# Early tokens' second matmul placed in the front, banks for second matmuls, and job DMAs on the sync queue, in an attention and mixture-of-experts kernel

## The chip, the cores and the metric

The kernel runs on one core of one Trainium2 chip. The metric is the device time of one execution in microseconds (us). Engines are named as in the profile: PE (TensorE matmul), PEld (TensorE weight load), DVE (VectorE), ACT (ScalarE), POOL (GpSimd), SP (SyncE); a "q" behind a name (PEldq, ACTq, SPq) means the sequencer, which issues DMAs and does branches and register loads.

## What is computed

The reference, cut to what matters:

```python
def _attn_ref(q, k, v):                      # (8 batches, 8 heads, 576 tokens, 64)
    q_s = softmax(q, axis=-1); k_s = softmax(k, axis=2)
    kv = np.einsum('bhsd,bhse->bhde', k_s, v)
    return np.einsum('bhsd,bhde->bhse', q_s, kv)

def _moe_ref(x, w_gate, w_output_gate, w1, w2):   # x: 4608 x 512, 8 experts, F = 1024
    e_idx = np.argmax(x @ w_gate, axis=1)
    gate_w = softmax(x @ w_gate)[arange, e_idx]; eom = sigmoid(x @ w_output_gate)
    for e in range(8):
        mask = e_idx == e
        ye = np.maximum(x[mask] @ w1[e], 0.0) @ w2[e]
        out[mask] = gate_w[mask, None] * eom[mask, e, None] * ye

def _moe2_ref(x, w_in, w_out):                    # 512 -> 2048 -> 512
    r = np.maximum(x @ w_in, 0.0)
    return (r * r) @ w_out

x = attn_out.transpose(0, 2, 1, 3).reshape(4608, 512)
return _moe2_ref(_moe_ref(x))
```

## The kernel before, in words

Three stages follow each other. The **front** (`front`, L84 to L560) computes the attention batch by batch and routes each token to one expert (`route_a`, `route_b`, `scatter`); the tokens go to `xd` in DRAM, and their places, ordered by expert, to `idl` and then `idbin`. The first 384 tokens that an early count gives to expert 0 ("early tokens") are gathered before the routing is finished, and their first matmul is done in the front (`early_mm`). At its end `window_sums` and `window_place` write the table `tab` (L621): for each of 19 windows its expert, its first token, its width (3: 384 columns, 2: 256, 0: none), and whether the next window changes the expert. All engines then read `tab` into registers (L634) and branch on it (`tc.If`).

The **windows** (`run`, `slot`, L766 to L945): slots 0 to 4 are skipped here, slots 5 to 18 run. A slot does, in this order: the first half of the second matmul (`mm2`, L695, 48 matmuls) of the window before; the transposes of its own tokens (`prep`, L675); the gather of the next window's tokens on POOL (L703); a few "ticks"; the second half of mm2; the output copies on ACT (`out_`, L858) and their stores; then its own first matmul (`mm1`, L681, 8 groups of 12) with `hook` after each group; then the scaling of the next tokens on POOL (`scale`, L700); at a change of expert the split of the next w1 (`split_w1`) and the load of its w2. A split (L630 on ACT, L631 on DVE) makes two fp32r parts, high and rest, of one fp32 tensor, so each product takes three passes. The load of w1 and the split of w2 stand in the hook after group 2. In this run experts begin at slots 5 (the early one), 7, 9, 10, 12 and 14; the widths of slots 5 to 18 are 384, 384, 384, 256, 256, 384, 256, 384, 256, 384, 384, 384, 384, 256.

**Ticks** (`tick`, L804) turn w_in and w_out from a 64-bit form into fp32, 64 jobs of 256 columns. Job j's data comes by `job_load` (256 KB into one of four `cv_s`); DVE does six operations (L818 to L827) on `ca` and `cb`, POOL one (L825), ACT a Square (L810); a job goes through ticks j and j+1. The first 32 jobs (w_in) are then stored to `wid_d` (L806), in tick j+2; the other 32 become `wO` in SBUF. Slots 7 to 12 have six ticks, slots 13 to 18 five: three (two) between the halves of mm2, three in the hooks after groups 1, 4 and 6. Loads and stores of jobs are issued on ACT's queue; SP's queue issues the weight loads.

**PSUM**: eight banks. mm1's groups and mm2's four outputs take turns in five of them, and `prep` uses the other three:

```python
pm = bank[(12 * i + f) % 5]                               # mm1, group f of slot i
pm = [bank[(12 * i + 8 + c) % 5] for c in range(KC)]      # mm2
```

The **end** (L946 to L1000) is the dense second layer, from `yd`, twelve times 384 tokens.

The order in each engine's queue is the order in which the program issues: nothing reorders it. What the change touches is the end of `front`, `early_mm`, `job_load`, `tick`, `mm1`, `mm2`, `out_` and `slot`.

## Time and profile before

| | us |
|---|---|
| median of 3 runs | 1545.45 (1543.21 to 1545.7) |
| the profiled execution | 1553.64 |
| its span | 1551.8 |
| PE busy | 1439.6 (93%) |
| DVE busy | 657.5 (42%) |
| ACT busy | 499.3 (32%) |
| POOL busy | 304.2 (20%) |

The mean granted clock of PE is 0.964 of full speed. Times inside the trace count from the start of the span. The span is 1.8 us shorter than its own execution's time, and that execution is 8.2 us longer than the median of the runs. Busy time of PE is modelled: consecutive groups of matmuls overlap by some tenths of a us, so the distance from one start to the next is the better duration.

### The profile page before, as it was taken

How to read it: one execution, taken by the hardware profiler on the slowest of the kernel's cores; microseconds unless marked ns; L12 is line 12 of the kernel's file. 1: busy time of each engine (PE TensorE's matmuls, PEld its weight loads, DVE VectorE, ACT ScalarE, POOL GpSimd, SP SyncE). 2: the span in 40 equal slices, each digit the busy share in tenths (PEclk: the TensorE clock that was granted, in tenths of full speed). 3: DMA queues.
4: the chain of work that ended last, by engine and by line, in shares of the span. 5: the costliest groups of instructions: out<-in, count | busy, mean ns of one | idle time of the engine just before them, and what ended most of it. 6: DMA issues, size and time to landing. Idle time of an engine off the chain costs nothing.

```text
span 1551.8 us, 21664 instructions
## 1 busy us (share of the span) xinstructions
PE 1439.6 (93%) x8180; PEld 1352.8 (87%) x8180; DVE 657.5 (42%) x1302; ACT 499.3 (32%) x1004; POOL 304.2 (20%) x315
## 2 busy tenths in 40 slices
PE   6999649998678799999999999999999999999998
PEld 6888549998678789999999999999999999999997
DVE  4455651267555666444532434223343232433322
ACT  4566421233333334333522323222232222322222
POOL 1244641134224265443000000000000000000000
PEclk9999879999889899999999999999999999999999
DMA  8564624367675746332520101001010100100000
GB/s 311 187 242 182 165 76 97 48 200 152 179 191 121 192 121 145 103 102 51 149 69 14 42 0 41 19 23 41 1 42 0 41 34 8 41 1 21 8 15 21
DMA packets 62220, 135.61 MB, mean 87 GB/s; under 512 B 13360, under 2 KB 31920, under 8 KB 58096
## 3 DMA queue, kind: packets, MB, share of 16 engines
q1 hardware_dynamic: 31200, 79.13, 15.9%
q10 hardware_dynamic: 22752, 32.99, 9.1%
q0 software_dynamic: 8112, 21.47, 4.5%
q8 instruction: 91, 1.49, 0.4%
q14 instruction: 65, 0.53, 0.1%
HBM read 98.36 MB, written 35.20 MB: 86 GB/s over the span
## 4 chain that ended last, share of the span: by engine, by line
PE 75%; DMA 4%; DVE 2%; issue 2%; ACT 1%; ACTq 0%; POOL 0%; POOLq 0%; DVEq 0%; PEldq 0%
PE bank L972 26%; PE bank L993 25%; PE bank L681 12%; PE bank L695 11%; DMA wid_d<-cv_a 3%; DMA raw<-moe_w 1%; PE bank L675 1%; DVE wA L631 1%; ACT yb L858 0%; DVE cv_a L819 0%; POOL xr L700 0%; DVE cv_b L824 0%; DMA out<-xr,idt 0%; DVE cv_a L827 0%; ACTq L799 0%
## 5 line engine op out<-in xcount | busy, mean ns | idle before, releaser
L993 PE MATMUL bank<-wO,h 128*128 128x512 f32 x1728 | 396.5, 390 | 0.0
L993 PEld LDWEIGHTS bank<-wO,h 128*128 128x128 f32 x1728 | 324.1, 188 | 66.4
L695 PE MATMUL bank<-h,wB 128*128 128x384 f32 (+1 forms) x1440 | 236.9, 324 | 24.4 <-issue 20.5
L681 PE MATMUL bank<-xT,wA 128*128 128x384 f32 (+1 forms) x1344 | 221.2, 328 | 35.8 <-ACT yb L858 26.2
L695 PEld LDWEIGHTS bank<-h,wB 128*128 128x128 f32 x1440 | 230.4, 195 | 25.7 <-issue 21.8
L681 PEld LDWEIGHTS bank<-xT,wA 128*128 128x128 f32 x1344 | 218.1, 199 | 37.1 <-ACT yb L858 27.5
L975 ACT ACTIVATE r<-bank 128x384 f32<-128x384 f32 x192 | 94.4, 492 | 443.2 <-PE bank L972 443.2
L977 DVE TENSOR_TENSOR gg<-r 128x384 f32<-128x384 f32 x192 | 107.3, 559 | 286.4 <-ACT r L975 286.2
L972 PE MATMUL bank<-xT,wB 128*128 128x384 f32 x1152 | 201.9, 334 | 0.0
L972 PE MATMUL bank<-xT,wA 128*128 128x384 f32 x1152 | 201.8, 336 | 0.0
L972 PEld LDWEIGHTS bank<-xT,wB 128*128 128x128 f32 x1152 | 200.3, 188 | 0.9
L972 PEld LDWEIGHTS bank<-xT,wA 128*128 128x128 f32 x1152 | 200.0, 188 | 1.0
L998 POOL DMA_INDIRECT out<-xr,idt x36 | 35.0, 974 | 770.9 <-DVE xr L997 765.9
L631 DVE TENSOR_TENSOR h<-gg,h 128x384 fp32r<-128x384 f32 x192 | 107.3, 559 | 111.5 <-ACT h L630 111.5
L630 ACT CAST h<-gg 128x384 fp32r<-128x384 f32 x192 | 98.7, 514 | 122.6 <-DVE gg L977 122.6
L685 DVE SCALAR_TENSOR_TENSOR h<-bank,h 128x384 fp32r<-128x384 f32 (+1 forms) x112 | 55.5, 506 | 103.2 <-ACT h L689 99.6
L825 POOL TENSOR_TENSOR cv_b<-cv_b,cv_e 128x256 f32<-128x256 f32 x64 | 52.6, 822 | 235.7 <-DVE cv_b L824 235.4
L997 DVE COPY xr<-bank 128x512 f32<-128x512 f32 x36 | 24.9, 692 | 123.7 <-PE bank L993 123.7
L689 ACT ACTIVATE h<-bank 128x384 fp32r<-128x384 f32 (+1 forms) x112 | 49.3, 452 | 79.0 <-PE bank L681 74.7
L810 ACT ACTIVATE cv_s<-cv_s 128x256 f32<-128x256 f32 x64 | 28.3, 443 | 117.8 <-DMA wid_d<-cv_a 45.4
L631 DVE TENSOR_TENSOR xT<-bank,xT 128x512 fp32r<-128x512 f32 x42 | 26.5, 683 | 85.8 <-ACT xT L630 85.8
L703 POOL DMA_INDIRECT xr<-xd,wid x45 | 44.6, 992 | 88.1 <-issue 71.3
(171 smaller groups left out, 1203.4 us busy)
## 6 DMA issues: line engine op xcount, KB each, us to landing
raw<-moe_w SPq DMA_DIRECT2D x52, 512.0 KB
yd<-yb ACTq DMA_DIRECT2D x56, 192.0 KB
raw<-yd SPq DMA_DIRECT2D x11, 768.0 KB
v<-v SPq DMA_DIRECT2D x8, 1024.0 KB
q<-q SPq DMA_DIRECT2D x8, 1024.0 KB
cv_s<-moe_w_in ACTq DMA_DIRECT2D x32, 256.0 KB
cv_s<-moe_w_out ACTq DMA_DIRECT2D x32, 256.0 KB
kt<-k SPq DMA_DIRECT2D x7, 1152.0 KB
```

Of the source, the lines that this page charges most:

```text
L630: nc.scalar.copy(out=hi, in_=src)
L631: (eng or V).tensor_tensor(out=lo, in0=src, in1=hi.bitcast(F32), op=ALU.subtract)
L681: nc.tensor.matmul(out=pm, lhsT=wA[a][:, c, f * P:(f + 1) * P], rhs=xT[b][:, c, 0:n], start=c == 0 and (a, b) == (0, 0), stop=c == KC - 1 ...
L685: V.scalar_tensor_tensor(out=h[1], in0=pm, scalar=0.0, in1=h[0].bitcast(F32), op0=ALU.max, op1=ALU.subtract)
L689: nc.scalar.activation(out=h[0], in_=pm, func=AF.Relu)
L695: nc.tensor.matmul(out=pm[c], lhsT=wB[a][:, f, c * P:(c + 1) * P], rhs=h[b], start=f == 0 and (a, b) == (0, 0), stop=f == 7 and a == 1)
L703: nc.gpsimd.indirect_dma_start(out=xr[j], out_offset=None, in_=xd[0:n], in_offset=bass.IndirectOffsetOnAxis(ap=wid[i % 2][:, j:j + 1], axi ...
L825: G.tensor_tensor(out=b.bitcast(F32), in0=b.bitcast(F32), in1=ce.bitcast(F32), op=ALU.subtract)
L972: nc.tensor.matmul(out=pm, lhsT=wi(a, 8 * hf + f)[:, c], rhs=yhl[b][:, c], start=c == 0 and (a, b) == (0, 0), stop=c == KC - 1 and a == 1)
L975: nc.scalar.activation(out=r, in_=pm, func=AF.Relu)
L977: V.tensor_tensor(out=gg, in0=r, in1=r, op=ALU.mult)
L993: nc.tensor.matmul(out=pm, lhsT=g[a][f][:, u * P:(u + 1) * P], rhs=wO[b][:, 8 * hf + f, :], start=hf == 0 and f == 0 and (a, b) == (0, 0), ...
```

## The change

It has four parts. In the front, the pieces of the w1 and w2 splits are issued in other places, the early tokens' transposes and first matmul earlier, in banks of the pool of `pt` tiles, and their second matmul (96 matmuls into four new banks `acc`) before the register loads of `tab`. In the slots, mm2 always writes the four `acc` banks, mm1 takes turns in the other four, and `prep` in three of those; no slot does the early window's mm2. Loads and stores of jobs go to SP's queue, `ca` has four buffers, `b` is written in place in `cv_s`, `ce` has two buffers, the store of a job is issued in tick j+1 instead of j+2, and loads three ahead instead of two. The scaling of the next tokens comes before mm1 instead of after it.

```diff
@@ front, from batch 6 on @@
         x_mm(n, 1)
         kv_m(n + 1)
         x_t(n, 3)
+        moe.split_w1([0], V)
         x_mm(n, 2)
+        moe.split_w1([1], V)
         x_mm(n, 3)
...
+        moe.split_w1([2], V)
         route_b(full)
-        moe.split_w1([0], V)
         x_mm(n, 1)
+        x_t(n, 3)
         route_b2(full)
         scatter(full)
-        x_t(n, 3)
-        route_a(late)
-        moe.split_w1([1], V)
+        moe.split_w1([3], V)
+        moe.load_w2(0)
         x_mm(n, 2)
         x_t(n, 4)
-        route_a1(late)
-        route_a2(late)
-        moe.split_w1([2, 3], V)
+        route_a(late)
         rctx.close()
         moe.open_down()
         moe.early_open()
-        moe.load_w2(0)
+        moe.early_prep(ps_t)
         x_mm(n, 3)
+        route_a1(late)
+        x_mm(n, 4)
+        route_a2(late)
...
+        moe.open_acc()
+        em, st = moe.early_mm(ps_t)
+        em(1)
+        route_a(last)
+        em(1)
...
         route_b(late)
         route_b2(late)
         scatter(late)
-        moe.early_prep(ps_t)
-        x_mm(n, 4)
-        moe.split_w2([0], V)
...
-        window_sums(tc, scratch, cst, pc, spec, wq)
+        moe.split_w2([0], V)
         em(1)
         st(1)
...
+        window_sums(tc, scratch, cst, wt_cnt, spec, wq)
         st(1)
-        moe.split_w2([1, 2, 3], V)
+        moe.split_w2([1], V)
+        em(1)
+        window_place(tc, scratch, cst, wq, tab, lambda: None)
+        em(1)
+        moe.split_w2([2, 3], V)
         moe.gather(MAXW)
+        em(6)
         regs = moe.regs()
@@ early_mm @@
+    def open_acc():
+        ap = octx.enter_context(tc.tile_pool(name="m_acc", bufs=1, space=PSUM, side="right", reuse_waits="tile"))
+        acc.extend(ap.tile([P, 512], F32, name=f"acc{i}") for i in range(KC))
...
+            for f in range(8):
+                mm2_f(f, [x[:, 0:EW] for x in acc], [h[f] for h in hT])
                 yield
@@ run: banks and buffers @@
-        bank.extend(ps.tile([P, 512], F32, name=f"bank{i}") for i in range(8))
+        bank.extend(ps.tile([P, 512], F32, name=f"bank{i}") for i in range(4))
+        bank.extend(acc)
...
-            ca = [cv.tile([P, CW], I32, name=f"cv_a{i}") for i in range(3)]
-            cb = [cv.tile([P, CW], I32, name=f"cv_b{i}") for i in range(2)]
-            ce = cv.tile([P, CW], I32, name="cv_e")
+            ca = [cv.tile([P, CW], I32, name=f"cv_a{i}") for i in range(NA)]
+            ce_ = [cv.tile([P, CW], I32, name=f"cv_e{i}") for i in range(2)]
@@ job_load, tick @@
-                    nc.scalar.dma_start(out=cs_[j % 4].rearrange("p a b -> p (a b)"), in_=(w_in if j < NI else w_out)[job_at(j)].bitcast(I32))
+                    nc.sync.dma_start(out=cs_[j % 4].rearrange("p a b -> p (a b)"), in_=(w_in if j < NI else w_out)[job_at(j)].bitcast(I32))
...
-                if done and u < NI:
-                    A.dma_start(out=wid_d[job_at(u)], in_=ca[u % 3].bitcast(F32))
-                job_load(j + 2)
...
-                    a, b = ca[j % 3], cb[j % 2]
+                    a, b, ce = ca[j % NA], lo_, ce_[j % 2]
...
                     V.scalar_tensor_tensor(out=a0, in0=m0, scalar=HMIN * HMIN, in1=a0, op0=ALU.is_ge, op1=ALU.mult)
+                    if k < NI:
+                        nc.sync.dma_start(out=wid_d[job_at(k)], in_=a0)
+                job_load(j + 3)
@@ prep, mm1, mm2, slot @@
-                    prep_tile(j, bank[5 + j].rearrange("p (c n) -> p c n", c=KC))
+                    prep_tile(j, bank[1 + j].rearrange("p (c n) -> p c n", c=KC))
...
-                    pm = bank[(12 * i + f) % 5]
+                    pm = bank[f % 4]
...
-                with tc.If(v_ == 2) as br:
+                with tc.If(v_ == 3):
+                    go(TW)
+                with tc.If(v_ == 2):
                     go(256)
-                with br.Else():
-                    go(TW)
...
-            for x in bank[0:5]:
-                V.memset(x[:, 256:TW], 0.0)
...
-                mm2(i - 1, range(4), vp)
+                if i:
+                    mm2(range(4), vp)
                 prep()
...
-                out_(i - 1, st, ys)
+                out_(st, ys)
+                if i + 1 < MAXW:
+                    scale(i + 1)
                 with tc.If(v_ == 3) as br:
                     mm1(i, TW, hook)
...
-                    scale(i + 1)
```

Where this stands in the engines' queues. On PE, at the end of the front, before: the last early first matmul (into `pe`), the register loads of `tab`, the branches over the skipped slots, and then the early tokens' second matmul (L695) in slot 5.

```order
L681 MATMUL pe_1772<-xT_1662,wA_1381 128x384
L865 UNCONDITIONAL_BRANCH
L634 TENSOR_LOAD tab x4
L932 COMPARE_AND_BRANCH
L634 TENSOR_LOAD tab
L929 COMPARE_AND_BRANCH
L848 UNCONDITIONAL_BRANCH
L695 MATMUL bank_2130<-h_0_1667,wB_1660 128x384
```

After, in the same place (line numbers are 3 to 8 higher): the second matmul's last row stands ahead of the loads, and the transposes of slot 5 come directly behind the branches.

```order
L698 MATMUL acc_1739<-h_7_1657,wB_1644 128x384
L637 TENSOR_LOAD tab x4
L940 COMPARE_AND_BRANCH
L637 TENSOR_LOAD tab
L937 COMPARE_AND_BRANCH
L678 MATMUL bank_2231<-ident,xr_1384 128x128 x4
L678 MATMUL bank_2232<-ident,xr_1385 128x128 x4
L678 MATMUL bank_2233<-ident,xr_1386 128x128 x4
L923 COMPARE_AND_BRANCH
L684 MATMUL bank_2230<-xT_1645,wA_1380 128x384
```

So the second matmul moved from behind the branches to before them; one branch (L848 before, L923 now) moved behind the transposes.

On ACT, in a slot with three ticks between the halves of mm2, before: the tokens' split (L630), then stores and loads of jobs and the Squares, and the output copy L858 behind them all.

```order
L630 CAST xT_1662<-bank_2128 128x4x128
L806 DMA wid_d<-cv_a_2144 128x256
L799 DMA cv_s_2139<-moe_w_in 128x512
L810 ACTIVATE cv_s_2140<-cv_s_2140 128x256
L806 DMA wid_d<-cv_a_2145 128x256
L848 UNCONDITIONAL_BRANCH
L799 DMA cv_s_2140<-moe_w_in 128x512
L810 ACTIVATE cv_s_2141<-cv_s_2141 128x256
L806 DMA wid_d<-cv_a_2143 128x256
L799 DMA cv_s_2141<-moe_w_in 128x512
L810 ACTIVATE cv_s_2142<-cv_s_2142 128x256
L858 COPY yb<-bank_2131 128x384
```

After, on SP: the same stores (L835) and loads (L808), with the weight loads (L660, w1) of a change of expert behind them in the same queue.

```order
L835 DMA wid_d<-cv_a_2244 128x256
L808 DMA cv_s_2240<-moe_w_in 128x512
L835 DMA wid_d<-cv_a_2245 128x256
L808 DMA cv_s_2241<-moe_w_in 128x512
L923 COMPARE_AND_BRANCH
L897 UNCONDITIONAL_BRANCH
L835 DMA wid_d<-cv_a_2246 128x256
L808 DMA cv_s_2242<-moe_w_in 128x512
L900 COMPARE_AND_BRANCH
L660 ISA
L660 DMA raw<-moe_w 128x1024
```

Between ACT's L630 and its output copy (now L865) only the Squares (L816) are left.

## Rows read from the trace of the kernel before

**Rows 1.** Table of stretches, from 348 us: start:end, length, busy us (instructions) by engine, clock, DMA share, GB/s.

```profile
348.00:600.00 252.00, 204.98 (x1347) 201.26 (x1346) 155.04 (x330) 93.98 (x180) 97.19 (x101) 0.89 0.64 159
600.00:752.00 152.00, 151.22 (x949) 150.47 (x947) 74.78 (x179) 52.01 (x116) 56.78 (x70) 1.00 0.41 114
```

**Rows 2.** PE's timeline where the front ends: start, length, tile, count [idle before, releaser].

```profile
233.59 10.79 PE L695 MATMUL bank<-h,wB 128*128 128x384 f32 x48 [20.53 <-issue]
...
245.44 8.57 PE L695 MATMUL bank<-h,wB 128*128 128x384 f32 x48
253.85 6.41 PE L681 MATMUL bank<-xT,wA 128*128 128x384 f32 x36
```

**Rows 3.** Views of lines L932, L929, L848: PE's sequencer, duration ns min/median/max.

```profile
L932 PEldq COMPARE_BRANCH  x1: 3553/3553/3553, 219.6 to 219.6; - x1
...
L929 PEldq COMPARE_BRANCH  x3: 70/83/6412, 223.5 to 268.0; - x3
...
L848 PEldq COMPARE_BRANCH  x38: 63/221/2261, 231.2 to 750.0; - x38
```

**Rows 4.** Timeline of all engines, around the table of windows.

```profile
189.97 0.59 ACT L630 CAST xT<-pt 128x512 fp32r<-128x512 f32 x1 [5.95 <-remote]
...
216.45 0.17 DVE L621 CAST tab<-wt 128x7 int32<-128x7 f32 x1
...
217.00 3.48 DVE L631 TENSOR_TENSOR wB<-raw,wB 128x1024 fp32r<-128x1024 f32 x3
...
229.35 2.04 POOL L700 TENSOR_TENSOR xr<-xr 128x512 f32<-128x512 f32 x2 [3.35 <-DMA xr<-xd,wid]
```

**Rows 5.** PE's timeline, 348 to 600 us.

```profile
363.18 12.35 PE L681 MATMUL bank<-xT,wA 128*128 128x256 f32 x84 [3.86 <-ACT yb L858]
...
399.83 13.96 PE L681 MATMUL bank<-xT,wA 128*128 128x256 f32 x94 [9.59 <-issue]
...
558.86 11.43 PE L681 MATMUL bank<-xT,wA 128*128 128x256 f32 x96
570.13 5.92 PE L695 MATMUL bank<-h,wB 128*128 128x256 f32 x48
...
581.41 8.28 PE L695 MATMUL bank<-h,wB 128*128 128x256 f32 x48
```

**Rows 6.** Waits, 348 to 600 us: who for whom, total us, times, longest us.

```profile
ACT cv_s L810 <- DMA wid_d<-cv_a: 43.6, 5, 13.7
DVE cv_a L818 <- DMA wid_d<-cv_a: 39.4, 12, 7.6
...
PE bank L681 <- ACT yb L858: 26.2, 4, 9.5
...
PE bank L675 <- POOL xr L700: 8.1, 7, 1.3
```

**Rows 7.** Timeline of all engines, 384 to 402 us: ACT's tick work.

```profile
399.39 0.43 ACT L810 ACTIVATE cv_s<-cv_s 128x256 f32<-128x256 f32 x1 [13.71 <-DMA wid_d<-cv_a]
```

**Rows 8.** Waits of SP's queue, 348 to 600 us.

```profile
SPq L657 <- DMA wid_d<-cv_a: 43.8, 3, 15.4
```

**Rows 9.** Groups of instructions, 348 to 600 us: count, busy us, mean ns, idle before.

```profile
L825 POOL TENSOR_TENSOR cv_b<-cv_b,cv_e 128x256 f32<-128x256 f32 x38 | 31.0, 817 | 144.2 <-DVE cv_b L824 144.0
...
L631 DVE TENSOR_TENSOR wA<-raw,wA 128x1024 fp32r<-128x1024 f32 x16 | 29.1, 1878 | 0.0
...
L631 DVE TENSOR_TENSOR wB<-raw,wB 128x1024 fp32r<-128x1024 f32 x14 | 17.0, 1273 | 0.4 <-ACT wB L630 0.3
...
L824 DVE SCALAR_TENSOR_TENSOR cv_b<-cv_s,cv_e 128x256 int32<-128x256 int32 x38 | 16.2, 425 | 1.3
...
L818 DVE TENSOR_SCALAR cv_a<-cv_s 128x256 int32<-128x256 int32 x38 | 11.0, 290 | 43.6 <-DMA wid_d<-cv_a 39.4 <-POOL wO L829 4.2
```

**Rows 10.** Groups of instructions, 234 to 348 us.

```profile
L631 DVE TENSOR_TENSOR wA<-raw,wA 128x1024 fp32r<-128x1024 f32 x4 | 4.6, 1220 | 0.6 <-ACT wA L630 0.6
```

**Rows 11.** Chain that ended last, 330 to 620 us: start, length, what.

```profile
507.51 13.21 DMA raw<-moe_w
```

More of the change, by code (lines that the diff above doesn't have):

```diff
@@ L515, in front @@
         xctx.close()
-        pse = pool("f_pse", 1, pctx, space=PSUM, reuse_waits="tile")
-        pe = [pse.tile([P, 512], F32, name=f"pe{i}") for i in range(4)]
-        em, st = moe.early_mm(pe)
+        moe.open_acc()
+        em, st = moe.early_mm(ps_t)
         spec = scratch([NE])
-        V.memset(spec, 0.0)
         em(1)
         route_a(last)
+        em(1)
+        V.memset(spec, 0.0)
+        st(1)
+        route_b(late)
+        route_b2(late)
+        scatter(late)
         em(1)
@@ L534, in front @@
             nc.tensor.matmul(out=pc, lhsT=chf[:, H_1:H_1 + P], rhs=onb[:, t], start=t == 0, stop=t == 5)
+        wt_cnt = scratch([NE])
+        V.tensor_copy(out=wt_cnt, in_=pc)
         pf = ps_t.tile([P, 1], F32, name="pt")
         nc.tensor.matmul(out=pf, lhsT=chf[:, H_1:H_1 + P], rhs=early1, start=True, stop=True)
+        V.tensor_scalar(out=spec[:, 0:1], in0=pf, scalar1=float(EW), scalar2=float(EW), op0=ALU.is_ge, op1=ALU.mult)
         route_b2(last)
@@ L544, in front @@
         st(1)
-        V.tensor_scalar(out=spec[:, 0:1], in0=pf, scalar1=float(EW), scalar2=float(EW), op0=ALU.is_ge, op1=ALU.mult)
-        window_sums(tc, scratch, cst, pc, spec, wq)
+        moe.split_w2([0], V)
         em(1)
         st(1)
-        def mid():
-            em(1)
-            st(1)
-        window_place(tc, scratch, cst, wq, tab, mid)
+        window_sums(tc, scratch, cst, wt_cnt, spec, wq)
         st(1)
-        moe.split_w2([1, 2, 3], V)
+        moe.split_w2([1], V)
[3 more added lines that the diff above has]
+        moe.split_w2([2, 3], V)
         moe.gather(MAXW)
+        em(6)
         regs = moe.regs()
@@ L634, in reg @@
         return nc.values_load(tab[i:i + 1, c:c + 1], engines=engines, min_val=0, max_val=mx)
-    wA, wB, wO, xT, wq, bank, wid, xr, hT = ([] for _ in range(9))
+    wA, wB, wO, xT, wq, bank, acc, wid, xr, hT = ([] for _ in range(10))
     raw = raw2 = None
@@ L734, in steps @@
                 h = [x[f] for x in hT]
[L735 removed]
+                pm = pp.tile([P, 512], F32, name="pt")[:, 0:EW]
                 mm1_pe(f, EW, pm)
@@ L832, in prep, with mm2, out_ @@
                 for j in range(3):
-                    prep_tile(j, bank[5 + j].rearrange("p (c n) -> p c n", c=KC))
+                    prep_tile(j, bank[1 + j].rearrange("p (c n) -> p c n", c=KC))
             def mm1(i, n, hook):
                 for f in range(8):
-                    pm = bank[(12 * i + f) % 5]
+                    pm = bank[f % 4]
                     mm1_f(f, n, pm[:, 0:n], [h[f][:, 0:n] for h in hT])
                     hook(f)
-            def mm2(i, fs, v_):
-                pm = [bank[(12 * i + 8 + c) % 5] for c in range(KC)]
+            def mm2(fs, v_):
                 def go(n):
                     for f in fs:
-                        mm2_f(f, [x[:, 0:n] for x in pm], [h[f][:, 0:n] for h in hT])
-                with tc.If(v_ == 2) as br:
+                        mm2_f(f, [x[:, 0:n] for x in acc], [h[f][:, 0:n] for h in hT])
+                with tc.If(v_ == 3):
+                    go(TW)
+                with tc.If(v_ == 2):
                     go(256)
-                with br.Else():
-                    go(TW)
             def store(st, c, y):
                 nc.scalar.dma_start(out=yd[c * P:(c + 1) * P, ds(st, TW)], in_=y)
-            def out_(i, st, yt):
+            def out_(st, yt):
                 for c in range(KC):
-                    nc.scalar.copy(out=yt[c], in_=bank[(12 * i + 8 + c) % 5][:, 0:TW])
+                    nc.scalar.copy(out=yt[c], in_=acc[c][:, 0:TW])
                     if st is not None:
                         store(st, c, yt[c])
-            for x in bank[0:5]:
-                V.memset(x[:, 256:TW], 0.0)
             e0, vh, vs = regs
@@ L873, in run @@
             yhl = xT
-            for j in range(2):
+            for j in range(3):
                 job_load(j)
@@ L911, in slot @@
                         tick(first + j)
-                mm2(i - 1, range(4, 8), vp)
-                out_(i - 1, st, ys)
+                if i:
+                    mm2(range(4, 8), vp)
+                out_(st, ys)
+                if i + 1 < MAXW:
+                    scale(i + 1)
                 with tc.If(v_ == 3) as br:
@@ L947, in run @@
             split_y(y0)
-            mm2(i, range(8), v_)
+            mm2(range(8), v_)
             yt = [x[:, 0:TW] for x in xr] + [cs_[0].rearrange("p a b -> p (a b)").bitcast(F32)[:, 0:TW]]
-            out_(i, None, yt)
+            out_(None, yt)
             for c in range(KC):
```

16 lines of the change are left out of this document (6 added, 10 removed).

## The prediction

> **What bounds the kernel now.** I read the table of stretches first, because the share of the whole span (PE busy 93%) hides where PE stands still. From 600 to 752 us PE is busy 151.22 of 152 us at clock 1.00, and after 752 it never lacks work: nothing is to be gained there. Two stretches are different: a hole of 20 us where the front ends, and 348 to 600 us, where PE works 204.98 of 252.00 us at clock 0.89 [rows 1].
>
> Then PE's own timeline around the hole [rows 2]. PE has ended the early tokens' first matmul, stands 20.53 us (from 213.06) with the releaser "issue", starts their second matmul (L695) at 233.59, runs its first half in 10.79 us where the second half, the same 48 matmuls, takes 8.57, and reaches slot 5's own first matmul at 253.85. "Issue" means that no data was awaited; the views of the branch lines say what was [rows 3]: on PE's weight-load sequencer, L932 cost 3.553 us once, and the longest of L929 and of L848 6.412 and 2.261 us. With the register loads of tab, these three lead from the table (cast at 216.45, done 216.62, [rows 4]) to 233.59, which is 17.0 us. The early tokens' second matmul needs nothing of that table.
>
> For the second stretch, again PE's timeline [rows 5], and the waits [rows 6]. 252.00 less 204.98 is 47.0 us of standing still. The largest part is bank <- ACT yb L858, 26.2 us in 4 waits; the 9.59 us that stand as "issue" at 399.83 have the same shape (two matmuls of a window, then a hole), so I count 36 us. These are first matmuls of a window that want a bank which ACT's output copy has not emptied. Why ACT is late: its Square L810 is put down to wid_d <- cv_a for 43.6 us in 5 waits, DVE's L818 for 39.4 us in 12; the one of 13.71 us ended at 399.39 [rows 7], 0.44 us before PE resumed at 399.83. So an in-order ACT holds tick work and tick DMAs ahead of the copies that PE waits for, and those DMAs wait for a store or a load to land. The rest: POOL scale L700 8.1 us, and a few us of DVE's h.
>
> Each hole is followed by slow matmuls. The 84 at 363.18 took 12.35 us and the 94 at 399.83 took 13.96, where 96 take 11.27 at full clock (558.86 to 570.13); the 48 at 581.41 took 8.28 against 5.9 [rows 5]. There are seven such stretches from 363.18 to 581.41, of 2.0 to 2.9 us each: about 16.4 us. So at most 47.0 + 16.4 = 63 us can be won in the middle.
>
> **The change part by part.**
>
> *Early second matmul in the front.* PE's rows change place: 96 matmuls move ahead of the register loads. They take 2 x 8.41 = 16.8 us at full clock (245.44 to 253.85 is one half, [rows 2]). They need the early h, and the w2 split. Before, three split pieces end at 217.00 + 3.48 = 220.48 [rows 4]; after, piece [1] stands ahead of the table, pieces [2] and [3] behind it, 1.2 us each. DVE's work in sum is the same, so without other gains the last piece would still end near 220.5; as the w1 splits are spread over stretches where DVE waited, I take 3 us less, 217.3, and 216 for piece [2] (a choice; without it all below is 3 us later). The last half of the early matmuls (f = 4 to 7, 8.4 us) needs these two pieces, so PE ends them near 224.3. PE's sequencer prepares ahead of PE; I take 3.3 us, an estimate of one and a half groups of 12 matmuls (2.1 us each by the same rows), so the loads start near 221.0, where they started at 216.6. From there the old 17.0 us, less 2.3 for the L848 branch, which now comes behind the transposes, set the transposes to 221.0 + 14.7 = 235.7, and with 1.1 us of them (between the halves, 244.38 to 245.44) and the 2.3 us branch the first matmul of slot 5 stands at 239 to 240. I take 239.8. Against 253.85 that is **14 us** won. Bounds: if the three branches were hidden beside the early matmuls, all of 20.5 us; if the waits of 186 to 192 us (ACT's xT cast stood 5.95 us, "remote", [rows 4]) come back in the new order and delay the mm2, 8 us or, if all of it is passed on, 0. Slot 5's transposes also need the gathers' scaled tokens, whose scales end at 229.35 + 2.04 = 231.4 [rows 4]; that is before 235.7 and hides.
>
> *Second matmuls in banks of their own.* Slot i's mm1 no longer asks for a bank that the output copy of slot i-1 empties; the copies get a whole mm1 (11 to 17 us) of room. The 36 us of yb waits go. What is late next: mm1 now has 4 banks instead of 5, so a late `h` residual stops PE after 3 groups of 1.4 to 2.1 us, not after 4; that is a dearer stall only where DVE lags, see below. The five memsets of the bank columns go; they stood on DVE while PE stood still for the branches, so I cost them at nothing, now as then.
>
> *Jobs on SP, four ca buffers, loads three ahead.* 32 stores and 64 loads leave ACT's queue; ACT no longer issues these 96, which is off the path by itself. The store of job k goes out one tick earlier, right behind DVE's last operation, and is due only four ticks after its buffer was taken, where it was three. The waits of 43.6 and 39.4 us shrink to those that a store of more than two ticks makes. SP is in order too: behind a weight load that waits for raw, loads and stores of jobs now queue. In the trace SP stood up to 15.4 us in L657 behind a wid_d store, 43.8 us in 3 waits [rows 8]. In program order those waits end when DVE has split the piece, and DVE does its ticks behind the splits, so most of it is covered; the rest is the slower rival. POOL's subtract now reads and writes every second element (in place in cv_s). No row shows it strided. Between no change and twice its dense 0.82 us (an estimate, [rows 9]) it costs POOL up to 31 us over 38 jobs, and POOL is busy 97.19 of 252 us [rows 1]; DVE uses the result a tick later. I cost it at nothing.
>
> *scale before mm1.* The w1 split costs DVE 1.878 us a piece here [rows 9], with the POOL scale beside it; 1.22 us in the stretch before, without [rows 10]. The scale moves into the mm2 phase, ahead of the splits, and 16 pieces x 0.66 = 10.5 us of DVE time comes back. PE's 8.1 us of waits for the scale go as well.
>
> *What stays in the middle.* At an expert change DVE has, in one window: w1 split 4 x 1.22 = 4.9, w2 split 4 x 1.273 = 5.1, tokens 2.0, residuals 4, and 6 ticks of 4 x 0.42 + 2 x 0.29 = 2.26 (L819, L821, L824, L827 like L824; L818 and L823 alike) = 13.6 [rows 9]: some 29.5 us. A window at 256 columns between two of 256 gives PE 11.3 + 2 x 5.9 + 1.1 = 24.2 us, 5.3 too little; where one of the two is 384 wide PE has 5.5 more, just even, with order and a late weight load (13.21 us for raw on the chain at 507.51, [rows 11]) against it. For four such changes (slots 9, 10, 12, 14) I keep 4 us each, 16 us, and 6 us of low clock behind them. 63 - 16 - 6 = 41; with the small hole past 600 us **42 us** won.
>
> **Sum.** 14 + 42 = 56. The profiled execution took 1553.64 us (span 1551.8); the median of the runs is 1545.45, 8 us below. 1545.45 - 56 = 1489. The best case, 20.5 + 63, is 1462.
>
> [...] The trace shows jobs and weights sharing the 16 engines: DMA share 0.64 in the middle, 0.41 after it [rows 1]. [...]
>
> **Rivals.** (1) *DVE and the landing of data become the bound.* Ticks still wait for stores (39.4 us on DVE's side alone, [rows 6]); with the banks free, late ticks delay residuals and so mm1. For it: DVE's waits on stores alone are nearly as long as PE's 47 us. Against it: the stores have a tick more, and four banks bridge 6 us. It would leave half of the middle's gain: 1545.5 - 14 - 21 = **1510**. (2) *The front gains nothing:* the branch chain only starts later, by what the new order delays the early matmul (the 5.95 us wait, the w2 pieces), and slot 5 begins at 253 as before; also the case in which the early matmul is issued early but does not run early. 1545.5 - 42 = **1503**. (3) *Slower: SP's order.* A 2 MB weight load stands ahead of job loads in the one ring; if the first tick of a group waits for it, DVE stops, and with it residuals and PE. Slots 7 to 12 have 12 groups of ticks; at 8.6 us each (half of the longest wait of 15.4 is 7.7, the raw load on the chain took 13.21; I take a value between) the 56 us are gone when 7 groups wait, and all twelve give 12 x 8.6 = 103, that is 1489 + 103 = 1592; at nine, 1489 + 77 = **1566**. Against it: three loads are out ahead, and only four changes of expert have weights to load there, so nine groups are hard to reach. [...]
>
> **Chances.** Forecast (both terms within some 12 us) 0.57; rival 1 0.16; rival 2 0.12; both at once, 1545.5 - 21 = 1524, 0.04; slower 0.04; no change, where pieces cancel, 0.03; better than the forecast's own range (branches hidden, changes of expert clean) 0.04. A difference of 0.2% (3 us) is what measuring this kernel can tell from none, as its runs spread from 1543.21 to 1545.7. The range takes in the forecast and rivals 1 and 2: 1467 to 1518. Faster 0.93, same 0.03, slower 0.04.
>
> **What would show it.** Front: L698 (the early mm2) before the table's loads and done near 224; the first transposes near 236, mm1 of slot 5 near 240, with the three long branches still there. Middle: no wait of PE for yb; clock near 0.95; PE's remaining holes at slots 9, 10, 12 and 14 with releaser h or raw; the w1 split back near 1.2 us. After the middle, the same work to the microsecond. Wrong would be: PE holes named after a DMA of cv_s or wid_d, SP waits of 8 us and more in front of L808, or an early mm2 that still starts after 216 and ends after 233.

## The result

The changed kernel takes 1496.49 us (median of 4 runs, 1495.24 to 1497.77), the kernel before 1544.33 us in the same comparison (4 runs, 1542.78 to 1545.7). The ratio is 0.9691, with a 95% interval from 0.9674 to 0.9707: 48 us less. A second comparison, on another chip, gave 0.9704 (0.9678 to 0.9731), so the ratio repeats.

The direction was right and the time lies in the stated range; the forecast of 1489 was 7.5 us too low. That the sum came so near is in part luck: the largest gain was put down to the banks, which alone gave nothing, and the queue, which was priced at nothing by itself, turned out to be needed for more than half of the middle's gain.

**The profile after.** The table of stretches of the changed kernel, columns as in [rows 1]. The window slots now reach the dense layer at 694 us instead of 752, so the stretch to set against 348 to 600 ends near 560.

```profile
330.00:560.00 230.00, 216.26 (x1483) 211.21 (x1482) 167.52 (x361) 98.88 (x196) 100.65 (x113) 0.99 0.65 188
560.00:700.00 140.00, 137.33 (x856) 135.01 (x855) 66.22 (x152) 47.54 (x105) 45.26 (x56) 1.00 0.36 106
```

In the first, PE stands 13.7 us instead of 47.0, and its clock is 0.99 instead of 0.89. In the second it is worse than before: 2.7 us of standing still, where 0.8 stood in 152 us.

PE's timeline where the front ends, against [rows 2]:

```profile
210.53 8.25 PE L698 MATMUL acc<-h,wB 128*128 128x384 f32 x46 [1.12 <-DVE wB L634]
228.75 2.79 PE L678 MATMUL bank<-ident,xr 128*128 128x128 f32 x12 [9.97 <-PEq L857]
```

The second half of the early tokens' second matmul ends at 218.78, then PE stands 9.97 us for the branches, and the twelve transposes take 2.79 us. Slot 5's first matmul follows at 233.32. Three long branches, against [rows 3], from the views of their lines:

```profile
L940 PEldq COMPARE_BRANCH  x1: 4063/4063/4063, 217.3 to 217.3; - x1
...
L937 PEldq COMPARE_BRANCH  x3: 70/83/4632, 221.8 to 249.1; - x3
...
L855 PEldq COMPARE_BRANCH  x47: 63/169/3267, 227.7 to 680.0; - x47
```

The first two jump over whole skipped slots; such branches (L932 and L929 before) took 3.6 to 6.4 us in the traces of the kernel before, the change, e6 and e12, where the median of PE's branches is 0.07 to 0.3. The third is the skipped If of slot 5's second matmul: L855 took 0.24 us at 227.7, ahead of the transposes, and 3.27 us at 229.2, behind them. So the branch that stands behind the transposes is L855; L923, which the section on the change names there, took 0.07 us. In the stretches of the three long branches (217.3 to 221.4, 221.8 to 226.4 and 229.2 to 232.5 us) the DMA view of the change counts 6, 3 and 1 packets on the queues that it calls "instruction"; from 226.4 to 229.2 us, where PE's branches took 0.07 to 0.24 us, it counts none. Whether the branches waited for these packets is not shown.

PE's timeline of the middle, against [rows 5], at a slot of 256 columns after a change of expert, at one of 384, and at one cycle of a quiet stretch:

```profile
382.61 2.34 PE L684 MATMUL bank<-xT,wA 128*128 128x256 f32 x12 [3.42 <-DVE h L688]
...
410.90 10.37 PE L684 MATMUL bank<-xT,wA 128*128 128x384 f32 x48 [3.00 <-DVE h L688]
...
588.99 1.50 PE L678 MATMUL bank<-ident,xr 128*128 128x128 f32 x12 [0.36 <-PEq L857]
...
599.13 16.91 PE L684 MATMUL bank<-xT,wA 128*128 128x384 f32 x96 [0.31 <-PEq L857]
...
634.83 16.91 PE L684 MATMUL bank<-xT,wA 128*128 128x384 f32 x96 [0.31 <-PEq L857]
```

The holes of 9 us are gone; slots 9 and 10 wait for DVE's h. What is new are two gaps of 0.3 to 0.6 us in nearly every slot: behind the second matmul's halves, with the releaser "PEq L857" (the end of the second If), where the window before is 384 wide, and ahead of them, mostly with "PEq L855" (the end of the first If), where it is 256 wide. From 599.13 to 634.83 a quiet slot of 384 columns takes 35.70 us. In the kernel before the same cycle took 34.64 us (660.06 to 694.70 in its PE timeline). That is 1.1 us per slot which the prediction had not counted at all. From 252 to 694 us the waits with these two names add up to 8.0 us:

```profile
PE bank L684 <- PEq L857: 3.1, 8, 0.6
PE bank L678 <- PEq L857: 3.0, 9, 0.5
PE acc L698 <- PEq L855: 1.9, 6, 0.3
```

The waits, 330 to 560 us, against [rows 6]: no wait of ACT or DVE for a wid_d store is left.

```profile
PE bank L684 <- DVE h L688: 6.4, 2, 3.4
PE bank L684 <- ACT yb L865: 1.7, 1, 1.7
```

### The profile page after: what moved, and what is told of

It reads as the page before. It is cut to its first block, busy times and chain, and to the rows that moved or that the text cites. A ratio compares the mean times of both kernels' runs of the same rounds, so it can differ in the third digit from the quotient of the medians.

```text
span 1493.6 us, 21934 instructions
## 1 busy us (share of the span) xinstructions
PE 1426.8 (96%) x8180; PEld 1334.7 (89%) x8180; DVE 661.8 (44%) x1298; ACT 496.1 (33%) x1004; POOL 296.8 (20%) x315
## 2 busy tenths in 40 slices
DMA packets 62221, 135.62 MB, mean 91 GB/s; under 512 B 13360, under 2 KB 31920, under 8 KB 58096
## 3 DMA queue, kind: packets, MB, share of 16 engines
q1 hardware_dynamic: 45024, 100.11, 21.1%
## 4 chain that ended last, share of the span: by engine, by line
PE 53%; issue 0%; DMA 0%; POOLq 0%; DVE 0%
PE acc L1001 26%; PE bank L980 23%; PE acc L980 3%; PE acc L698 1%; DMA out<-xr,idt 0%; POOLq L1055 0%; DVE xr L1005 0%; POOLq L1006 0%
## 5 line engine op out<-in xcount | busy, mean ns | idle before, releaser
L1001 PE MATMUL acc<-wO,h 128*128 128x512 f32 x1728 | 396.5, 390 | 0.0
L1001 PEld LDWEIGHTS acc<-wO,h 128*128 128x128 f32 x1728 | 324.1, 188 | 66.4
L698 PE MATMUL acc<-h,wB 128*128 128x384 f32 (+1 forms) x1440 | 232.1, 319 | 5.7 <-DVE wB L634 2.1
L698 PEld LDWEIGHTS acc<-h,wB 128*128 128x128 f32 x1440 | 225.1, 190 | 8.8 <-issue 4.1
L684 PEld LDWEIGHTS bank<-xT,wA 128*128 128x128 f32 x1344 | 209.7, 191 | 17.3 <-issue 7.8
L980 PE MATMUL bank<-xT,wB 128*128 128x384 f32 x1008 | 178.9, 334 | 0.0
L980 PE MATMUL bank<-xT,wA 128*128 128x384 f32 x1008 | 178.7, 336 | 0.0
L980 PEld LDWEIGHTS bank<-xT,wB 128*128 128x128 f32 x1008 | 175.5, 188 | 0.9
L980 PEld LDWEIGHTS bank<-xT,wA 128*128 128x128 f32 x1008 | 175.2, 188 | 0.9
L831 POOL TENSOR_TENSOR cv_s<-cv_s,cv_e 128x256 f32<-128x256 f32 x64 | 54.1, 845 | 159.4 <-DVE cv_s L830 159.2
L1005 DVE COPY xr<-acc 128x512 f32<-128x512 f32 x36 | 24.9, 691 | 124.1 <-PE acc L1001 124.1
```

The source lines that it names most:

```text
L684: nc.tensor.matmul(out=pm, lhsT=wA[a][:, c, f * P:(f + 1) * P], rhs=xT[b][:, c, 0:n], start=c == 0 and (a, b) == (0, 0), stop=c == KC - 1 ...
L698: nc.tensor.matmul(out=pm[c], lhsT=wB[a][:, f, c * P:(c + 1) * P], rhs=h[b], start=f == 0 and (a, b) == (0, 0), stop=f == 7 and a == 1)
L831: G.tensor_tensor(out=b.bitcast(F32), in0=b.bitcast(F32), in1=ce.bitcast(F32), op=ALU.subtract)
L980: nc.tensor.matmul(out=pm, lhsT=wi(a, 8 * hf + f)[:, c], rhs=yhl[b][:, c], start=c == 0 and (a, b) == (0, 0), stop=c == KC - 1 and a == 1)
L1001: nc.tensor.matmul(out=pm, lhsT=g[a][f][:, u * P:(u + 1) * P], rhs=wO[b][:, 8 * hf + f, :], start=hf == 0 and f == 0 and (a, b) == (0, 0), ...
```

## The stages, kernel by kernel

The profiles' chips differ: the kernel before took 1540 to 1552 us on those used here, and its front (the same code) wrote `tab` at 216.4 us in the profile of [rows 4] and at 204 to 207 on others. So stages are compared between chips only with that in mind. The table gives, from each trace, when `tab` was written, when slot 5's first matmul ended, and how long it took from there to the first matmul of the dense layer (the middle: slots 6 to 18 and the last second matmul). Behind that, the traces agree (792.5 to 793.2 us to the last matmul).

| kernel | tab | slot 5's mm1 ends | middle | ratio to before |
|---|---|---|---|---|
| before | 216.4 | 270.7 | 481.5 | 1 |
| e8 banks alone | 207.1 | 260.2 | 478.9 | 0.9996 |
| e9 jobs alone | 205.4 | 259.7 | 451.6 | 0.9834 |
| e10 jobs and scale | 204.2 | 259.2 | 434.2 | 0.9696 |
| e11 jobs, scale, banks | 207.0 | 260.3 | 432.5 | 0.9687 |
| the change | 209.2 | 251.7 | 442.4 | 0.9691 |
| e5 the change again | 206.9 | 249.4 | 440.6 | 0.9704 |
| e7 no early mm2, Else | 206.2 | 256.7 | 440.2 | 0.9741 |
| e6 Else | 208.1 | 250.8 | 441.7 | 0.9691 |
| e12 wide first | 208.2 | 250.4 | 427.1 | 0.9601 |
| e1 Else, other chip | 216.0 | 261.7 | 437.4 | 0.9668 |
| e2 jobs on ACT | 215.2 | 256.8 | 468.8 | 0.9863 |
| e3 old ticks | 219.0 | 261.2 | 465.7 | 0.9832 |
| e4 scale late | 215.5 | 260.9 | 469.8 | 0.9832 |

The last four ran on the chip where the kernel before took 1552 us. Two traces of one kernel differ in the middle by 1.8 us (the change and e5) and by 4.3 us (e1 and e6), so less than that says nothing.

## The experiments

**e1, e6: the If with an Else again.** In the changed kernel, for slots 8 to 18 and the last second matmul:

```diff
-                with tc.If(v_ == 3):
-                    go(TW)
-                with tc.If(v_ == 2):
+                with tc.If(v_ == 2) as br:
                     go(256)
+                with br.Else():
+                    go(TW)
```

> The changed kernel, with the second matmul of slots 8 to 18 in one If with an Else again instead of two Ifs, banks and all else as changed. Theory A (a skipped If ends in semaphore updates for which PE's sequencer first lets the matmuls run out, so each half of the second matmul and the start of the next stage costs PE 0.3 to 0.5 us): 11 slots lose some 1.1 us each, so about 12 us less than the changed kernel, 1484 us, and no gap of PE named after the If lines in slots 8 to 18. Theory B (the gaps come with any branch, or with the banks): within 3 us of the changed kernel's 1496.5.

> The same kernel as e1, now beside the changed kernel on one chip. Theory A (each skipped If costs PE a drain; its trace showed a cycle of 34.63 us where the changed kernel's has 35.75): 8 to 12 us less than the changed kernel. Theory B (the time comes back elsewhere, in fetches of code or in DVE): within 3 us of it.

e1: 1498.98 us, ratio 0.9668 (0.9623 to 0.9714), beside a kernel before of 1551.81. e6: 1493.83 us, ratio 0.9691 (0.9664 to 0.9718), beside 1540.98 and beside e5, the change itself, at 1496.29. So 2.5 us, within the uncertainty: by its time, theory B. The trace shows why, and that the drain is real. PE's timeline of e6:

```profile
325.46 9.90 PE L698 MATMUL acc<-h,wB 128*128 128x384 f32 x48 [2.99 <-issue]
...
545.79 10.62 PE L698 MATMUL acc<-h,wB 128*128 128x384 f32 x48 [5.11 <-issue]
...
565.89 16.81 PE L684 MATMUL bank<-xT,wA 128*128 128x384 f32 x96
...
600.52 9.70 PE L684 MATMUL bank<-xT,wA 128*128 128x384 f32 x55
```

From 565.89 to 600.52 the quiet cycle is 34.63 us again, and no gap is named after the If. In exchange PE stands 2.99 and 5.11 us for "issue" in front of second matmuls, with slow matmuls behind (10.62 us where 8.5 is usual). From 251 to 692 us these waits, and the view of the If's line with the branch that was late, are:

```profile
PE acc L698 <- issue: 8.3, 3, 5.1
...
L856 PEldq COMPARE_BRANCH  x32: 63/212/6222, 320.6 to 690.4; - x32
```

Its long cases, 4.75 us at 320.6 and 6.22 at 539.5, with one of 4.79 us in the first matmul's If (L929) at 367.0, stand at the same slots in e1 (4.74, 5.58, 4.95) and in e7 (5.52, 5.64, 3.93). The middle came out at 441.7 us (437.4 in e1), against 442.4 and 440.6 with the two Ifs: most or all of what the drains had cost was given back to late branches. In e6 each of the three falls close behind the issue of a weight load (314.9 to 319.0, 360.2 to 363.6 and 533.9 to 537.9 us), with the DMA share at 0.98 to 1.04 (last number but one):

```profile
320.60:325.40 4.80, 1.87 (x11) 1.55 (x9) 3.86 (x11) 1.14 (x3) 1.90 (x3) 0.95 1.01 391
367.00:371.80 4.80, 2.09 (x18) 1.89 (x16) 4.66 (x13) 1.77 (x4) 1.46 (x2) 1.00 1.04 394
539.50:545.70 6.20, 1.17 (x7) 0.85 (x5) 4.45 (x12) 0.82 (x2) 3.20 (x5) 0.81 0.98 360
```

No run moved a weight load to test whether the late branches hang on it; that they hang on how the If is written is what e12 shows.

**e5: the change again.** No edit.

> The changed kernel itself, unaltered, on the chip that runs the next kernels, as their yardstick. The kernel before took 1544 us on one chip and 1552 on another, so the ratio is what should repeat: 0.967 to 0.971 of the kernel before.

1496.29 us (1491.09 to 1499.01), ratio 0.9704. As expected.

**e2: jobs' DMAs on ACT's queue.**

```diff
-                    nc.sync.dma_start(out=cs_[j % 4].rearrange("p a b -> p (a b)"), in_=(w_in if j < NI else w_out)[job_at(j)].bitcast(I32))
+                    nc.scalar.dma_start(out=cs_[j % 4].rearrange("p a b -> p (a b)"), in_=(w_in if j < NI else w_out)[job_at(j)].bitcast(I32))
...
-                        nc.sync.dma_start(out=wid_d[job_at(k)], in_=a0)
+                        A.dma_start(out=wid_d[job_at(k)], in_=a0)
```

> The changed kernel, with the job loads and stores issued on ACT's queue instead of SP's, at the same points of the program and with the same buffers. Theory A (banks of their own removed the waits; the queue matters little): 1496 to 1502 us. Theory B (ACT standing in front of job DMAs was the cause): 15 to 35 us slower, with h and the output copies of ACT late, and PE waits for DVE's h or for yb.

1529.7 us, ratio 0.9863 (0.984 to 0.9885); by the change's ratios of 0.969 to 0.970 it would have been 1504 to 1506 on this chip, so 24 to 26 us slower: theory B. The change itself was not run on this chip, and the interval of the ratio is worth some 4 us either way; but the middle of the trace is 26 to 28 us longer than the change's as well. ACT's waits in the middle (330 to 600 us), and PE's:

```profile
ACT h L692 <- POOL cv_s L831: 27.6, 8, 4.6
...
PE bank L684 <- DVE h L688: 25.1, 7, 7.8
```

A job's load on ACT waits until POOL and DVE have let go of its buffer, and its store until DVE's last operation; behind it in ACT's queue stands the Relu that makes h, and behind that DVE's residual and PE: the Relu's waits are 27.6 us for POOL's L831 and 9.4 us for DVE's L833. In the change PE's waits for h are 6.4 us. The buffers and the number of bytes are those of the change.

**e3: ticks, buffers and queue as before.**

```diff
-            ca = [cv.tile([P, CW], I32, name=f"cv_a{i}") for i in range(NA)]
-            ce_ = [cv.tile([P, CW], I32, name=f"cv_e{i}") for i in range(2)]
+            ca = [cv.tile([P, CW], I32, name=f"cv_a{i}") for i in range(3)]
+            cb = [cv.tile([P, CW], I32, name=f"cv_b{i}") for i in range(2)]
+            ce = cv.tile([P, CW], I32, name="cv_e")
...
+                if done and u < NI:
+                    A.dma_start(out=wid_d[job_at(u)], in_=ca[u % 3].bitcast(F32))
+                job_load(j + 2)
...
```

> The changed kernel, with job loads, ticks and buffers as in the kernel before (ACT's queue, three ca, two cb, one ce, store in the tick after next, loads two ahead). Theory A (banks alone gave most): up to 8 us slower than the changed kernel. Theory B (buffers and queue gave most): 20 to 35 us slower; the waits of ACT and DVE on the wid_d stores come back with 40 us each and now delay h instead of yb.

1527.15 us, ratio 0.9832 (0.9809 to 0.9856), some 22 us slower than the change would be there: theory B, though the waits on the stores came back at 21.4 and 16.8 us, half of what was expected, beside 54.5 us of ACT's Square put down to weight loads. As e2 costs the same with the new buffers, the fourth buffer and the earlier store bring nothing while the DMAs stand on ACT's queue. The reverse, SP's queue with the old buffers and order, was not run, so whether the queue alone is enough stays open.

**e4: the scale behind the first matmul again.**

```diff
-                if i + 1 < MAXW:
-                    scale(i + 1)
                 with tc.If(v_ == 3) as br:
...
                 if i + 1 < MAXW:
+                    scale(i + 1)
                     ch = reg(i + 1, 4, [ENG.Activation, ENG.DVE, ENG.SP], 2)
```

> The changed kernel, with the scaling of the next tokens behind the first matmul again. Theory A (POOL's scale beside DVE's split stretches the split of w1 from 1.2 to 1.9 us a piece, and the transposes wait for it): 5 to 12 us slower, w1 split at 1.8 us or more in the middle, PE waits for the scale of some 6 us. Theory B (both are covered): within 3 us.

1526.89 us, ratio 0.9832 (0.9809 to 0.9854): some 22 us slower, the mechanism of theory A at about twice its price. The w1 split's row in the middle of e4 (330 to 590 us):

```profile
L703 POOL TENSOR_TENSOR xr<-xr 128x512 f32<-128x512 f32 x24 | 36.2, 1534 | 0.0
...
L634 DVE TENSOR_TENSOR wA<-raw,wA 128x1024 fp32r<-128x1024 f32 x16 | 29.3, 1887 | 0.0
```

and the same rows of the change (330 to 560 us):

```profile
L703 POOL TENSOR_TENSOR xr<-xr 128x512 f32<-128x512 f32 x21 | 21.3, 1040 | 0.2 <-issue 0.2
...
L634 DVE TENSOR_TENSOR wA<-raw,wA 128x1024 fp32r<-128x1024 f32 x16 | 20.0, 1293 | 3.8 <-ACT wA L633 3.7
```

Both stretch by half when they run side by side: DVE works 16 x 0.59 = 9.5 us longer on the split. PE waits 7.2 us for the scale, where the change has no such wait, and 14.6 us for h (7.00 of them in one piece at slot 9), where the change has 6.4. The rest of the 22 us was not followed.

**e8: the banks alone**, in the kernel before.

```diff
-                    prep_tile(j, bank[5 + j].rearrange("p (c n) -> p c n", c=KC))
+                    prep_tile(j, bank[1 + j].rearrange("p (c n) -> p c n", c=KC))
...
-                    pm = bank[(12 * i + f) % 5]
+                    pm = bank[f % 4]
...
-                pm = [bank[(12 * i + 8 + c) % 5] for c in range(KC)]
+                pm = bank[4:8]
...
```

> The kernel before with the banks alone changed: first matmuls in four banks, second matmuls in four of their own, the transposes in three of the first; front, jobs and scale as before. Theory A (the prediction's: 36 us of waits for yb and the slow clock behind them go with the banks): 30 to 42 us faster than before. Theory B (the waits for yb were only where DVE's and ACT's lateness came to light; it comes out as waits for h): 5 to 15 us faster, with waits of PE for DVE's h of 15 us or more.

1540.24 us, ratio 0.9996 (0.9978 to 1.0014): nothing. Less than theory B's 5 us, and theory A is refuted. The waits of e8 (260 to 600 us):

```profile
DVE cv_a L818 <- DMA wid_d<-cv_a: 43.8, 13, 7.9
...
ACT cv_s L810 <- DMA wid_d<-cv_a: 39.0, 5, 14.3
...
PE bank L681 <- DVE h L685: 18.1, 5, 6.5
...
PE bank L681 <- ACT cv_s L810: 12.4, 2, 11.2
```

The waits on the stores are those of [rows 6], and PE waits for h where it waited for yb. The 11.2 us put down to ACT's Square are another thing: PE's own branch at slot 9's first matmul was late, from 376.0 to 389.1, and PE resumes at 389.14.

```profile
L914 PEldq COMPARE_BRANCH  x1: 13054/13054/13054, 376.0 to 376.0; - x1
```

The kernel before has a hole of that length in the same slot: the 9.59 us at 399.83 in [rows 5]. It stands after the 2nd of the 12 matmuls of one group, which all write the same bank, while the four yb waits stand after the 12th. So it was no wait for yb, and its cause is open. What e8 shows is that banks were not short: with ACT just as late, PE waits for h instead.

**e9, e10, e11: jobs; jobs and scale; jobs, scale and banks**, in the kernel before, each by the lines of the diff of the change.

> The kernel before with the jobs' part alone: loads and stores on SP, four ca, b in place, two ce, loads three ahead, stores one tick earlier; banks, scale and front as before. Theory A (the job DMAs on ACT were what made ACT late; the waits for yb go with them): 12 to 20 us faster than before, waits of PE for yb under 8 us in sum. Theory B (it takes banks too): within 5 us of before, with the waits for yb still there.

> e9 with the scale of the next tokens moved ahead of the first matmul as well; banks and front as before. Theory A (banks give nothing in the middle; jobs and scale give all of it together): 33 to 40 us faster than before, as e11. Theory B (with DVE and ACT on time the five shared banks are the next limit): 15 to 25 us faster, with PE waiting for yb.

> e10 with the banks of the change: the whole change but for its front. The second matmul keeps its If with an Else. Theory A: the middle gives 38 us, the front 9 to 10, so 36 to 40 us faster than before and 9 us slower than the whole change (ratio 0.975). Theory B (the front gives the 14 us and more that the prediction had): 28 to 34 us faster than before (ratio 0.980).

All three ran beside a kernel before of 1540.46 us. e9: 1512.86 us, ratio 0.9834 (0.9801 to 0.9867), 28 us, more than theory A's 20; PE's waits named yb are 2.8 us; the hole of slot 9 that stands as issue is still there, with 8.3 us. The scale was not touched yet, and shows it (e9, 330 to 600 us):

```profile
L700 POOL TENSOR_TENSOR xr<-xr 128x512 f32<-128x512 f32 x24 | 36.2, 1533 | 0.0
...
L631 DVE TENSOR_TENSOR wA<-raw,wA 128x1024 fp32r<-128x1024 f32 x16 | 29.3, 1887 | 0.0
```

e10: 1493.57 us, ratio 0.9696 (0.9667 to 0.9726), 19 us less again, with five shared banks: 47 us below the kernel before. It went beyond theory A's 40. Its waits in 262 to 600 us have next to nothing of yb (slot 9's hole is down to 4.1 us):

```profile
PE bank L681 <- ACT yb L858: 2.4, 2, 1.5
```

e11: 1492.77 us, ratio 0.9687 (0.9656 to 0.9718): the banks add nothing that can be told apart (0.8 us). Both theories for e11 had it slower than the whole change; it is as fast. So jobs and scale alone reach what the whole change reaches. The front's gain is in the traces of the change and e5 (slot 5's first matmul ends 7.5 to 10.9 us earlier than in e8 to e11), and so is a loss: their middle is 8 to 10 us longer than e11's. The second matmul's two Ifs are the difference in the slots' program, but with one If again the middle was hardly shorter (441.7 in e6, 437.4 in e1); e12 settles how far the form of the If matters.

**e7: no second matmul in the front** (e6, with the eight steps of `mm2_f` and three calls of `em` left out, and the If with an Else in all slots).

> e6 without the early tokens' second matmul in the front: slot 5 does it again, in the If with an Else; front order, banks and jobs as in the change. Theory A (the 96 matmuls fill a hole that is otherwise there): 14 to 19 us slower than e6, and slot 5's first matmul ends 14 to 19 us later. Theory B (most of the gain in the front came from the new order of splits and from the earlier table): at most 6 us slower.

1500.53 us, ratio 0.9741 (0.9714 to 0.9767), 6.7 us slower than e6; slot 5's first matmul ends 5.9 us later (256.7, 250.8). That is close to theory B. PE's timeline of e7:

```profile
220.33 10.08 PE L695 MATMUL acc<-h,wB 128*128 128x384 f32 x48 [24.07 <-DVEq L937]
```

The hole is 24 us and the matmuls that could fill it take 16.8. But the branches start only when PE's sequencer has handed out these matmuls: it reads `tab` at 206.4 us in e7, right behind the table, and at 214.5 in e6, and then PE stands another 9.9 us. So the hole shrinks by 14 us in PE's view, and slot 5 gains 6. The rest goes into a front that was 1.9 us later in e6, into 2.0 us of waits for the w2 split between the early matmuls, into 1 us behind the transposes, and into the slow clock, which in e6 falls on the transposes and on 96 matmuls of slot 5 (2.79 and 19.37 us, where 1.5 and 16.8 are usual; in the change, where they take 2.79 and 18.40 us, the granted clock is 0.50 from 223 to 236 us and 1.00 from 237). e7 pays some 1.6 us of that kind itself.

**e12: 384 columns first.** One If with an Else in all slots of the changed kernel, the wide case in the If:

```diff
-                with tc.If(v_ == 3):
-                    go(TW)
-                with tc.If(v_ == 2):
-                    go(256)
+                def pick():
+                    with tc.If(v_ == 3) as br:
+                        go(TW)
+                    with br.Else():
+                        go(256)
+
+                if sure:
+                    pick()
+                else:
+                    with tc.If(v_ > 0):
+                        pick()
...
```

> The changed kernel with the second matmul in one If with an Else in all slots, the 384 columns in the If and the 256 in the Else; up to slot 7 inside an If on there being a window before. Theory A (e1 and e6 lost the drains but got three late branches of 4 to 6 us by the jump over the 256 columns' code that stands first; here 384 runs on without that jump): 8 to 14 us faster than the change, ratio 0.960 to 0.965. Theory B (any form has such branches somewhere): ratio 0.967 to 0.971, with branches over 3 us on PE's sequencer at other places.

1478.82 us (1476.38 to 1479.68), ratio 0.9601 (0.9575 to 0.9627): faster than both kernels, 62 us below the kernel before, and 14 us below e11 on the same chip; theory A. From e12's profile, its front, one quiet cycle, and the longest branches in the first matmul's If:

```profile
227.27 2.79 PE L678 MATMUL bank<-ident,xr 128*128 128x128 f32 x12 [9.43 <-PEq L864]
231.12 19.27 PE L684 MATMUL bank<-xT,wA 128*128 128x384 f32 x96 [1.05 <-PEq L864]
```

```profile
585.41 16.81 PE L684 MATMUL bank<-xT,wA 128*128 128x384 f32 x96
...
620.05 16.81 PE L684 MATMUL bank<-xT,wA 128*128 128x384 f32 x96
```

```profile
L930 PEldq COMPARE_BRANCH  x23: 63/281/412, 231.0 to 651.8; - x23
```

The cycle is 34.64 us, and behind the front no branch of PE takes over 0.8 us. The middle is 427.1 us, 5 below e11's, and the front 10 us earlier: here the whole change pays. One thing goes beyond theory A: the late branch of the first matmul's If is gone too, though e12 leaves the order of its two cases as it was. So the jump alone does not explain the late branches; no run shows what does.

## Why the prediction was right, and where it was wrong

**The front, 14 us: mechanism right, size 8 to 11.** Slot 5's first matmul ended at 249.4 to 251.7 (the change, e5, e6, e12) against 259.2 to 260.3 (e8 to e11, front as before), 9.3 us earlier on average. The chain of loads and branches came out as worked: loads from 215.52 instead of 221.0 (3.3 us ahead of the end of PE's matmuls at 218.78, as estimated), 13.2 us to the transposes (14.7 forecast), 4.6 us to the first matmul. From the table to that matmul it took 24.1 us (209.2 to 233.3), and 37.4 before: 13.3 us won. What the step left out: PE had stood, and behind that the granted clock was 0.50 (in the change, from 223 to 236 us), so slot 5's 96 matmuls took 18.4 to 19.4 us instead of 16.8 (before, the second matmul paid that, [rows 2]). The new order also wrote the table some 1 to 2 us later, not earlier (206.2 to 208.2 in e5, e6, e7 and e12, against 204.2 to 207.1 in e8 to e11). Of the 3 us that the prediction chose for the splits, about half came: the last piece ends 2.3 us behind the table (at 211.61), where 0.7 was forecast and 3.9 stood before. And only 6 of the 9 us are the early second matmul (e7 against e6); some 3 came with the rest of the front (e7 against e8 to e11).

**The middle, 42 us: the size nearly right (37 to 41), by luck; three steps wrong.** The step "The 36 us of yb waits go", put down to the banks, failed: banks alone gave nothing (e8), and with jobs and scale moved the five shared banks cost nothing either (e10). The 36 were also misread: 9.59 of them were no wait for yb (see e8). The chain that the prediction itself had read (an in-order ACT with tick work and DMAs ahead of the copies) was the cause, and the part that removed it was the one on jobs: 28 us with its queue, buffers and order (e9), of which 24 to 26 are lost when the queue alone goes back to ACT (e2). The prediction said of the DMAs' leaving ACT that it "is off the path by itself".

The step on the scale was right in its mechanism: the split of w1 came back to 1.29 us a piece (1.2 forecast) and PE's waits for the scale went. Its 10.5 us of DVE and 8.1 us of PE's waits are 18.6 in sum; e9 to e10 measured 19.3. As these are times of two engines, the close match is partly chance. POOL's subtract on every second element, costed at nothing, took 0.845 us a piece (0.822 before).

The third step is one that is missing: the second matmul's two Ifs. The diff shows them and no term prices them. Their waits are 8.0 us in the change's trace. The If with an Else of e6 removes most of these waits and gains little or nothing, through late branches; e12, without drains and late branches, is 14 to 15 us shorter in the middle. So what has to be priced is the form of the If, and it is more than the Ifs' own waits. Against that error stands another: DVE's shortage at changes of expert was set at 22 us, with its slow clock, and e12's middle has 10 us of standing still in all (PE works 416.9 of its 427.1 us).

**The rivals.** The first (half of the middle's gain) did not come, nor the slower one, though job and weight transfers now stand on one queue (q1 moved 45024 packets, before 31200). But one of the prediction's signs of being wrong, SP waits of 8 us and more in front of L808, did appear (330 to 560 us):

```profile
SPq L808 <- DVE cv_a L833: 37.5, 9, 9.2
SPq L835 <- DVE cv_a L833: 26.0, 12, 5.7
SPq L835 <- DMA raw<-moe_w: 22.7, 9, 6.1
SPq L808 <- DMA raw<-moe_w: 20.2, 10, 4.7
```

SP waits longest behind DVE's operations, and 42.9 us are put down to weight loads; no row of PE names a load of a job, so these waits did not reach PE. The sign was badly chosen: it tells that SP waits, not that anything waits for SP. The second rival (the front gains nothing) did not come either, as the front was 8 to 11 us earlier; the whole change only came out no faster than e10 and e11 because its middle was longer.

**The queue.** The bytes (135.62 MB, before 135.61) and the DMA share of the middle (0.65, before 0.64) stayed the same, and the queue was worth 24 to 26 us (e2): what it moves is not the data but the waits in front of each issue, which on ACT hold up the work behind them (37.0 us of the Relu's waits in e2).

**Median and profile.** The profile of before was 8 us above the median of its runs. As `tab` was written 9 to 12 us later in it than in the same front on two other chips (204 to 207 us), that difference lies ahead of the table; the sum counts from the table on and is left alone. The front of the change shows the same spread: 207 to 209 us in the change and e5, 215 to 219 in e1 to e4, on the chip where the kernel before took 1552 us.

## What to carry to other kernels

A DMA that must wait for another engine belongs on the queue of an engine with nothing urgent behind it (24 to 26 us here, e2); look at what stands behind the issue, not at the issue's own time. When PE waits for a buffer, ask who is late with it before giving out more buffers: here banks of their own for the second matmuls were worth nothing, and taking work out of the late engines' way brought 47 us (e10). And price every control-flow line of a diff, in more than one form: between the change and e12 only the form of one If differs, and its 14 to 15 us are more than the new overlap in the front brought.

## What the runs showed that was not expected

- A skipped If costs PE a drain: in the change, the sequencer's semaphore update at L857 comes only when the matmuls ahead have run out (the branch at 595.79 takes 0.21 us, the update follows at 598.86), and PE then stands 0.3 to 0.5 us, twice a slot; 35.70 us a cycle instead of 34.64.
- The order of the two cases of one If, with the same work in them, decided some 13 us (e6 to e12, middle 441.7 and 427.1, less some 2 for the drains that e6 keeps in slots 6 and 7): three branches of 4.8 to 6.2 us, at fixed slots, in one, and none over 0.8 us in the other. In e6 all three fall under a weight load, with the DMA share at 0.98 to 1.04; whether that is the reason is open.
- POOL's scale and DVE's split, side by side, both took half as long again (1.04 to 1.53 us, 1.29 to 1.89 us).
- One branch of PE took 13.05 us in e8, the longest of all runs, and the profile gave the hole that it left to ACT's Square. Where a releaser looks odd, read the sequencer's own line.
